# Five small edits to the attention stage: the last head pair multiplies unrounded probabilities by unrounded V in one 32-bit product per step

## The chip, the cores and the metric

The kernel runs on one core of a Trainium2 chip. The metric is the device time of one execution in microseconds (us). TensorE is called PE here, its weight loads PEld, VectorE DVE, ScalarE ACT, GpSimd POOL; SP is the engine whose queue issues most DMAs. Each engine works through its own list of instructions in order and waits on semaphores for the others.

## The reference

Three stages follow each other. The first is attention over 2 x 8 heads with 1152 keys of 64 values; pairs of neighbouring queries are averaged, so that each head has 576 queries. Then come two feed-forward layers over 1152 tokens.

```python
q_pool = q.reshape(B, H, S // 2, 2, D).mean(axis=3)
scores = scale * np.matmul(q_pool, k.transpose(0, 1, 3, 2))
attn = np.exp(scores - np.max(scores, axis=-1, keepdims=True))
attn = attn / (np.sum(attn, axis=-1, keepdims=True) + 1e-09)
x = np.matmul(attn, v)                       # then tokens x 512
h = x @ w_in                                 # layer 1, 512 -> 2048
g = (a0 + a1*h + a2*h**2 + a3*h**3) / (1 + |b0|*|h| + |b1|*h**2 + 1e-6)
x = g @ w_out                                # back to 512
h = x @ w_in2
out = softplus(h) @ w_out2                   # layer 2
```

The layers' weights come as 64-bit floats and are turned into 32-bit ones on the chip.

## The kernel before

**Rounded products.** Nearly every product runs in the rounded 32-bit format fp32r (`F32R`). To keep the accuracy, an operand is split into a rounded part and the rounded rest, as `ph` and `pl` for the probabilities `p`, and three products are added: high by high, high by low, low by high.

**Attention in pairs.** Two heads make a pair; there are 8 pairs, numbered 0 to 7, and 36 steps per pair (`ST`). A step takes 128 keys and 288 queries: `s_step` forms the scores with two products (L446, L447) and ACT takes the exponential into `p` (L450). Every two steps `s_split` casts `p` into `ph` on ACT (L457) and subtracts into `pl`, on POOL for pairs 0 to 6 and on DVE for pair 7 (L122, the line of the helper `sub`). `pv` then adds three products per step into `pv` (L469 to L471). Nine steps make a group; `xev_a` divides its result (L479 to L485: two ACT and three DVE instructions) and `xev_b` splits it into `xh` (ACT, L492) and `xl` (POOL) for layer 1.

**The maximum of the next pair.** While pair j-1 takes its steps, `p1_fill` forms the scores of pair j a first time, only for their maxima: 9 tiles of 128 queries by 3 parts of 384 keys (units `u`, 27 in all), each two products (L396), and `p1_max` reduces each on DVE (L401). Tile 4 holds the last 64 queries of one head and the first 64 of the other and takes four products. `shift_a`, `shift_t`, `shift_m` turn the maxima into ten rows of `ql` (DVE, PE L418 into `ts`, DVE L425 and L432). The PSUM buffer of `ts` is one of three that the scores `s` also use, so a later `s_step` waits until DVE has read `ts`.

**Weights.** 64 tiles of weights, 512 KB each, are loaded by SP into two buffers `wraw`, and are converted: ACT (L176), three DVE instructions (L182, L185, L188; the middle one is left out at first), then an ACT cast (L198) and a DVE subtraction (L122) into `w`. Three of them come in the middle pairs, 14 from pair 6 on, among the steps; the rest during the layers. Layer 1 begins behind pair 7: `up` forms `h` in one of two PSUM buffers (L609, 24 products for two blocks), ACT applies three functions (L625 to L627), and DVE frees the buffer with L632 to L634.

**Order.** `at(t, fn, pr)` collects the work with a due step and a priority; the sorted list is traced, and the scheduler orders each engine's list from that.

Of the kernel before, what the change touches and what calls it, by code (L numbers as in the profile page):

```python
# [7 lines left out]
F32 = mybir.dt.float32  # L8
F32R = mybir.dt.float32r
# [8 lines left out]
T = dict(  # L18
    warm=24,
    wu=1,  # L20
    ft=2,
    lv=0,
    pv=15,
    pvd=8,
    pe=8,
    ped=3,
# [8 lines left out]
    q0=27,  # L35
# [51 lines left out]
def attn_moe_kernel(tc, q, k, v, w1_in, w1_out, moe_a, moe_b, w2_in, w2_out, out):  # L87
# [210 lines left out]
    def load_v(j):  # L298
# [5 lines left out]
        )  # L304
        st["vr", j] = vr

    def prep_v(j, x):
        v2, vr = V2[j % 2][:, x], st["vr", j][:, x]
        nc.scalar.copy(out=v2[:, :, 0:64], in_=vr)
        sub(nc.gpsimd if T["vl"] > x else nc.vector, v2[:, :, 128:192], vr, v2[:, :, 0:64])  # L310
# [60 lines left out]
            nc.sync.dma_start(out=QL[j % 2][x][64:74].bitcast(F32).rearrange("p (a b) -> p a b", b=128),  # L371
                              in_=zero[64:74].bitcast(F32).unsqueeze(1).to_broadcast([10, 5, 128]))

    def p1_fill(j, u):
        t, e = divmod(u, 3)
        i = j % 2
        if u == 0:
            st["nm", j] = late.tile([128, 9, 3], F32, tag="nm", name="nm", bufs=2)
        if j == 0 and u % 2:
            o = pps.tile([128, 512], F32, tag="s", name="p1")[:, 0:384]  # L380
        else:
            o = pp1.tile([128, 512], F32, tag="p1", name="p1")[:, 0:384]
# [12 lines left out]
        for a, (l, r) in enumerate(mm):
            m = nc.tensor.matmul(out=o, lhsT=l, rhs=r, start=(a == 0), stop=(a == len(mm) - 1))  # L396
        st["last", "pe"] = m.ins

    def p1_max(j, u):
        t, e = divmod(u, 3)  # L400
        nc.vector.tensor_reduce(out=st["nm", j][:, t, e:e + 1], in_=st.pop(("p1", j, u)), axis=AX.X,  # L401
                                op=ALU.max, negate=True)
# [36 lines left out]
    def s_step(j, s):  # L439
        g, c = divmod(s, C)  # L440
        x, half = divmod(g, 2)
        i = j % 2
        cs = qcols(x, half)
        ks = slice(c * 128, (c + 1) * 128)
        t = pps.tile([128, 512], F32, tag="s", name="s")[:, 0:HALF]
        nc.tensor.matmul(out=t, lhsT=KS[i][x][:, ks], rhs=QQ[i][x][:, cs], start=True, stop=False)  # L446
        nc.tensor.matmul(out=t, lhsT=KH[x][:, ks], rhs=QL[i][x][:, cs], start=False, stop=True)  # L447
        if s % 2 == 0:
            st["p"] = late.tile([128, 2, HALF], F32, tag="p", name="p", bufs=4)
        st["last", "exp"] = nc.scalar.activation(out=st["p"][:, s % 2], in_=t, func=AF.Exp).ins  # L450

    def s_split(j, s):
        p = st["pg", j, s]
        ph = late.tile([128, 2, HALF], F32R, tag="ph", name="ph", bufs=5)
        pl = late.tile([128, 2, HALF], F32R, tag="pl", name="pl", bufs=5)
        n = s // 2 + j * ST // 2
        nc.scalar.copy(out=ph, in_=p)  # L457
        sub(nc.vector if j == NP - 1 else nc.gpsimd, pl, p, ph)
        for e in range(2):
            st["ph", j, s - 1 + e] = (ph[:, e], pl[:, e])  # L460

    def pv(j, s):
        g, c = divmod(s, C)
        if c == 0:
            st["pv", j, g] = ppv.tile([128, 512], F32, tag="wm", name="pv")[:, 0:HALF]
        ph, pl = st.pop(("ph", j, s))
        v2 = V2[j % 2][:, g // 2]
        h, l = v2[:, c, 0:128], v2[:, c, 128:192]
        nc.tensor.matmul(out=st["pv", j, g], lhsT=h, rhs=ph, start=(c == 0), stop=False)  # L469
        nc.tensor.matmul(out=st["pv", j, g][0:64], lhsT=l, rhs=ph, start=False, stop=False)  # L470
        nc.tensor.matmul(out=st["pv", j, g], lhsT=h, rhs=pl, start=False, stop=(c == C - 1))  # L471
# [16 lines left out]
    def xev_b(j, g):  # L488
        c0 = (j // NPB) * SQ + (g % 2) * HALF
        o = (slice(None), j % NPB, slice(c0, c0 + HALF))  # L490
        xs = st.pop(("xs", g % 2))
        nc.scalar.copy(out=xh[o], in_=xs)  # L492
        sub(nc.gpsimd if T["xl"] else nc.vector, xl[o], xs, xh[o])

    def s_group(j, s):
# [4 lines left out]
    for j in range(NP):  # L500
        b0, b1, b2 = ST * j, ST * (j - 1), ST * (j - 2)
        A = lambda t, fn, *a, pr=0: at(t, lambda: fn(*a), pr)
        A(b1 + T["lv"], load_v, j)
        for x in range(2):
            if j == 0:
                A(b1 + T["v0"] + T["pvd"] * x, lambda x=x: behind(lambda: prep_v(0, x), "act", "dve"), pr=7)
            else:
                if j == 1 and T["vb"]:
                    A(b1 + T["pv"] + T["pvd"] * x, lambda x=x: behind(lambda: prep_v(1, x), "act", "dves"), pr=7)
                else:  # L510
                    A(b1 + (T["pv"] + T["pvd"] * x if j < NP - 1 else T["pe"] + T["ped"] * x), prep_v, j, x, pr=7)
        if j == 0:
            A(b2 + 0, first_load)
            A(b2 + 1, warm, T["warm"])
            for f, g in FIRST:
                A(b2 + 2, f, 0, g)
                A(b1 + T["ft"], lambda f=f, g=g: behind(lambda: f(1, g), "act", "dve"))
            A(b1 + T["ft"] + 1, lambda: behind(constants, "dve"))
            A(b1 + T["ft"] + 1, lambda: behind(moe_consts, "act", "dve"))
        else:  # L520
            o = b2 + (T["k1"] if j == 1 else 0)
            A(b2 + 0, load_kq, j)
            A(o + T["pq"], prep_q, j)
            for g in range(3):
                A(o + T["tk"] + T["tkd"] * g, tr_k, j, g, pr=1)
                if j == 1 and T["tb"] > 2 - g:
                    A(o + T["tk"] + T["tkd"] * g + T["tke"],
                      lambda g=g: behind(lambda: tr_k_ev(1, g), "act", "dves"), pr=2)
                else:
                    A(o + T["tk"] + T["tkd"] * g + T["tke"], tr_k_ev, j, g, pr=2)  # L530
            for g in range(2):
                A(o + T["tq"] + T["tqd"] * g, tr_q, j, g, pr=1)
                A(o + T["tq"] + T["tqd"] * g + T["tqe"], tr_q_ev, j, g, pr=2)
            A(o + T["ks0"], dma_ks, j, 0)
            A(o + T["q0"], dma_q, j, 0)
            A(o + T["ks1"], dma_ks, j, 1)
            A(o + T["q1"], dma_q, j, 1)
        A(b0 + T["kh0"], dma_kh, j, 0)
# [10 lines left out]
            A(t0 + T["p1m"], p1_max, j, u, pr=T["prm"])  # L549
        for x in range(2):  # L550
            t0 = b1 + T["s0"] if x == 0 else b1 + T["s1"]
            A(t0, shift_a, j, x)
            A(t0 + T[f"st{x}"], shift_t, j, x, pr=1)
            A(t0 + T[f"st{x}"] + T["sm"], shift_m, j, x, pr=2)
        for s in range(ST):
            A(b0 + s, s_step, j, s, pr=0)
            if s % 2 == 1:
                A(b0 + s, s_group, j, s, pr=1)
                A(b0 + s + T["sg"], s_split, j, s, pr=T["prs"])
            g, c = divmod(s, C)  # L560
            A(b0 + C * g + T["po"] + c * T["ps"] // 9, pv, j, s, pr=T["prp"])
        for g in range(4):
            A(b0 + C * g + T["xa"], xev_a, j, g, pr=T["pra"])
            if g >= 2:
                A(b0 + C * g + T["xb"], xev_b, j, g, pr=3)

    def pre(i, t0, lead, d, pool):
        at(t0, lambda: behind(lambda: w_load(i), "sp"))
# [17 lines left out]
    tc0 = ST * (NP - 2) + T["wc"]  # L586
    at(tc0, close_early)
    at(ST * (NP - 1) + T["ce"], close_even)
    for i in range(NRA + NRB):
        pre(NE + i, tc0 + 1 + T["wg"] * i, 4, 1, (lambda: st["wra"]) if i < NRA else (lambda: st["wrb"]))  # L590

    ph_ = pa_ = ap = wl_ = pt_ = pt2 = None
# [146 lines left out]

    if True:  # L740
        make_identity(nc, ident)
        nc.vector.memset(zero, 0.0)
        for i in range(2):
            nc.gpsimd.memset(V2[i][:, :, :, 64:128].bitcast(F32), -1.0)
# [17 lines left out]
        wl_ = sb(name="wlast", bufs=NW - NP1 - NE - NRA - NRB)  # L762
        pt_ = sb(name="part", bufs=1)

        freed = [wl_] * (NW - NP1 - NE - NRA - NRB)
        n0 = NE + NRA + NRB
        cnt = {"load": n0, "abs": n0, "conv": n0, "split": n0}

        def w_step():
# [150 lines left out]
```

## Time and profile before

| what | us |
|---|---|
| median of 3 runs (748.14 to 791.52) | 749.07 |
| the profiled execution | 748.41 |
| its span, first to last instruction | 746.6 |
| PE busy in the span | 725.7 (97%) |
| DVE, ACT, POOL busy | 551.6, 502.0, 227.2 |
| scores of pairs 6 and 7 begin | 256.68, 293.09 |
| last product of pair 7 begins | 333.74 |

A busy PE is not a PE at its peak, since matmuls overlap: what one costs is read from start to start in a row without waits. The share of the whole span is an average; pairs 0 to 6, pair 7, and the layers have different limits.

### The profile page before, as it was taken

Reading aid. Unit: us, or ns where it says so; the run is one execution under the profiler, and the core shown is the slowest. Engines: PE = TensorE matmul, PEld = TensorE weight load, DVE = VectorE, ACT = ScalarE, POOL = GpSimd, SP = SyncE. Lnnn points to the kernel's source line nnn. Section 1 sums busy time; section 2 is a strip of 40 time slices with the busy share of each in tenths; the row PEclk is TensorE's granted clock in tenths of the full one; section 3 lists DMA queues with packets and bytes.
Section 4 is the critical chain, followed back from the end, with each engine's and each line's share of the span. In section 5 each row is a group of like instructions: output and inputs, shape, how many; then the busy total and the mean of one; then the engine's idle time right before and its main releaser. Section 6 shows DMA issues by size and latency. Waiting matters only on the chain.

```text
span 746.6 us, 11768 instructions
## 1 busy us (share of the span) xinstructions
PE 725.7 (97%) x4273; PEld 683.5 (92%) x4273; DVE 551.6 (74%) x956; ACT 502.0 (67%) x967; POOL 227.2 (30%) x189
## 2 busy tenths in 40 slices
PE   8999999999999998887999999999999999999998
PEld 5699999999999998777999999999899998989896
DVE  5877777777777679998989999999987575611122
ACT  3278888888888889996767777787564454422221
POOL 5278787878787776000000000000000000000000
PEclk9999999999999999998999999999999999999999
DMA  4866373737353434432111221211124333101011
GB/s 131 207 151 151 96 183 87 179 87 182 87 120 96 92 101 125 141 113 84 57 58 57 67 75 56 86 58 56 38 80 137 110 117 107 63 1 43 0 43 43
DMA packets 60475, 70.33 MB, mean 94 GB/s; under 512 B 20008, under 2 KB 48512, under 8 KB 60416
## 3 DMA queue, kind: packets, MB, share of 16 engines
q1 hardware_dynamic: 59232, 68.58, 34.0%
q10 hardware_dynamic: 1184, 0.98, 0.4%
q8 instruction: 34, 0.56, 0.3%
q14 instruction: 25, 0.20, 0.1%
HBM read 47.71 MB, written 2.36 MB: 67 GB/s over the span
## 4 chain that ended last, share of the span: by engine, by line
PE 86%; DVE 7%; ACT 5%; issue 1%; POOL 0%; DVEq 0%; ACTq 0%
PE acc L712 13%; PE h L690 13%; PE p L396 11%; PE acc L658 11%; PE h L609 11%; PE s L446 5%; PE s L447 5%; PE pv L471 4%; PE pv L469 4%; PE pv L470 4%; ACT p L450 1%; ACT ph L457 1%; PE wm L264 1%; PE tk L327 1%; DVE w L122 1%
## 5 line engine op out<-in xcount | busy, mean ns | idle before, releaser
L122 POOL TENSOR_TENSOR pl<-p,ph 128x576 fp32r<-128x576 f32 x126 | 181.5, 1453 | 54.8 <-ACT ph L457 35.4
L401 DVE TENSOR_REDUCE nm<-p 128x1 f32<-128x384 f32 x216 | 117.0, 552 | 44.4 <-PE p L396 42.9
L450 ACT ACTIVATE p<-s 128x288 f32<-128x288 f32 x288 | 114.7, 407 | 29.2 <-PE s L447 27.6
L122 DVE TENSOR_TENSOR gl<-p,gh 128x384 fp32r<-128x384 f32 (+1 forms) x72 | 49.6, 689 | 93.3 <-ACT gh L699 92.3
L609 PE MATMUL h<-xh,w 128*128 128x384 f32 x384 | 100.8, 341 | 4.2 <-DVE p L633 4.2
L457 ACT CAST ph<-p 128x576 fp32r<-128x576 f32 x144 | 96.7, 671 | 2.4
L690 PE MATMUL h<-xh,w 128*128 128x384 f32 x384 | 97.8, 336 | 0.0
L698 ACT ACTIVATE p<-h 128x384 f32<-128x384 f32 x48 | 23.6, 492 | 109.5 <-PE h L690 109.4
L658 PE MATMUL acc<-gh,w 128*128 128x384 f32 x384 | 93.0, 337 | 1.0 <-ACT gh L619 1.0
L712 PE MATMUL acc<-w,gh 128*128 128x512 f32 x288 | 90.0, 394 | 0.0
L471 PE MATMUL pv<-pl,v 128*128 128x288 f32 x288 | 87.1, 303 | 1.7 <-DVE pl L122 1.3
L469 PE MATMUL pv<-ph,v 128*128 128x288 f32 x288 | 87.1, 303 | 1.2 <-ACT ph L457 1.0
L470 PE MATMUL pv<-ph,v 128*64 128x288 f32 x288 | 85.8, 298 | 0.0
L609 PEld LDWEIGHTS h<-xh,w 128*128 128x128 f32 x384 | 71.1, 192 | 4.5 <-issue 4.5
L690 PEld LDWEIGHTS h<-xh,w 128*128 128x128 f32 x384 | 70.2, 188 | 3.9
L658 PEld LDWEIGHTS acc<-gh,w 128*128 128x128 f32 x384 | 68.7, 188 | 2.1 <-ACT gh L619 2.0
L609 PE MATMUL h<-xl,w 128*128 128x384 f32 x192 | 65.3, 340 | 0.0
L690 PE MATMUL h<-xl,w 128*128 128x384 f32 x192 | 64.6, 337 | 0.0
L712 PEld LDWEIGHTS acc<-w,gh 128*128 128x128 f32 x288 | 53.5, 188 | 9.0
L658 PE MATMUL acc<-gl,w 128*128 128x384 f32 x192 | 59.7, 338 | 0.3 <-DVE gl L122 0.3
L471 PEld LDWEIGHTS pv<-pl,v 128*128 128x128 f32 x288 | 55.0, 191 | 5.0 <-DVE pl L122 3.9
L469 PEld LDWEIGHTS pv<-ph,v 128*128 128x128 f32 x288 | 55.6, 193 | 2.6 <-ACT ph L457 2.4
(152 smaller groups left out, 1620.6 us busy)
## 6 DMA issues: line engine op xcount, KB each, us to landing
wraw<-in_moe_w_in_dram SPq DMA_DIRECT2D x32, 512.0 KB
wraw<-in_moe_w_out_dram SPq DMA_DIRECT2D x32, 512.0 KB
vr<-in_v_dram SPq DMA_DIRECT2D x8, 576.0 KB
kr<-in_k_dram SPq DMA_DIRECT2D x15, 288.0 KB
qr<-in_q_dram SPq DMA_DIRECT2D x15, 256.0 KB
out_dram<-m SPq DMA_DIRECT2D x15, 128.0 KB
kha<-ks0a SPq DMA_DIRECT2D x4, 288.0 KB
khb<-ks0b SPq DMA_DIRECT2D x4, 288.0 KB
```

Of the source, the lines that this page charges most:

```text
L122: return eng.tensor_tensor(out=o, in0=a, in1=b, op=ALU.subtract)
L396: m = nc.tensor.matmul(out=o, lhsT=l, rhs=r, start=(a == 0), stop=(a == len(mm) - 1))
L401: nc.vector.tensor_reduce(out=st["nm", j][:, t, e:e + 1], in_=st.pop(("p1", j, u)), axis=AX.X, op=ALU.max, negate=True)
L450: st["last", "exp"] = nc.scalar.activation(out=st["p"][:, s % 2], in_=t, func=AF.Exp).ins
L457: nc.scalar.copy(out=ph, in_=p)
L469: nc.tensor.matmul(out=st["pv", j, g], lhsT=h, rhs=ph, start=(c == 0), stop=False)
L470: nc.tensor.matmul(out=st["pv", j, g][0:64], lhsT=l, rhs=ph, start=False, stop=False)
L471: nc.tensor.matmul(out=st["pv", j, g], lhsT=h, rhs=pl, start=False, stop=(c == C - 1))
L609: nc.tensor.matmul(out=h, lhsT=w[:, wi, wd], rhs=x[:, d, xcols(c)], start=(n == 0), stop=(n == 3 * ND - 1))
L658: nc.tensor.matmul(out=st["acc", c, d], lhsT=w[:, wi, wd], rhs=g, start=(first and n == 0), stop=(last and n == 2))
L690: nc.tensor.matmul(out=h, lhsT=w[:, wi, d * 128:(d + 1) * 128], rhs=x[:, d, xcols(c)], start=(n == 0), stop=(n == len(mm) - 1))
L712: nc.tensor.matmul(out=st["acc", c, t], lhsT=g[:, t * 128:(t + 1) * 128], rhs=w[:, wi], start=(first and n == 0), stop=(last and n == 2))
```

## The change

1. In pair 7 `s_step` writes the exponential into buffers with the tag `ph`, and `s_split` does nothing more. `pv` issues one product per step with both operands in plain 32-bit (`F32`), V from the new tiles `vf`. `load_vf` fills five of these straight from memory (V in columns 0 to 63, -1 in 64 to 127) in buffers of `p` and `pl`, which pair 7 has no other use for; the load and the split of V into `V2` fall away for pair 7.
2. Tile 4 of `p1_fill` takes three products for pairs 1 to 7, with the two heads' queries on the diagonal of the tiles `QD`, which four DMAs per pair fill (`dma_qd`); and tile 4 comes first (`unit`).
3. The three `shift` steps of pair 7 are traced in a high priority.
4. In pair 7 `pv`, `xev_a` and `xev_b` are due earlier, and the cast into `xh` is on POOL.
5. 13 weights in place of 14 are converted ahead of layer 1's start; the buffer of the 14th is the first to be used there.

```diff
+    QD = [late.tile([128, 128], F32R, name=f"qd{x}") for x in "hl"]
...
+    def load_vf(i):
+        b, h = (NP - 1) // NPB, 2 * ((NP - 1) % NPB)
+        if i < 4:
+            t = late.tile([128, 2, HALF], F32, tag="p", name="p", bufs=4)
+        else:
+            t = late.tile([128, 2, HALF], F32, tag="pl", name="pl", bufs=5)
+        t = t.rearrange("p a b -> p (a b)")[:, 0:512].rearrange("p (c e) -> p c e", c=4)
+        nc.gpsimd.memset(t[:, :, 64:128], -1.0)
...
+                nc.sync.dma_start(
+                    out=t[:, a - n0:z - n0, 0:64],
+                    in_=v[b, h + x].rearrange("(p c) d -> p c d", p=128)[:, a - x * C:z - x * C],
+                )
+        st["vf", i] = t
...
+    def dma_qd(j):
+        for d, n in zip(QD, ("qhi", "qlo")):
+            fcopy(d[0:64, 0:64], st[n, j][0:64, 512:576])
+            fcopy(d[64:128, 64:128], st[n, j][64:128, 0:64])
+
+    def unit(j, u):
+        return u if j == 0 else u + 12 if u < 3 else u - 3 if u < 15 else u
...
+        if j and t == 4:
+            mm = [(QD[0], st["khi", j][:, ks]), (QD[0], st["klo", j][:, ks]), (QD[1], st["khi", j][:, ks])]
+            srcs = []
...
         if s % 2 == 0:
-            st["p"] = late.tile([128, 2, HALF], F32, tag="p", name="p", bufs=4)
+            if j == NP - 1:
+                st["p"] = late.tile([128, 2, HALF], F32, tag="ph", name="ph", bufs=5)
+            else:
+                st["p"] = late.tile([128, 2, HALF], F32, tag="p", name="p", bufs=4)
...
     def s_split(j, s):
         p = st["pg", j, s]
+        if j == NP - 1:
+            for e in range(2):
+                st["ph", j, s - 1 + e] = (p[:, e], None)
+            return
...
-        sub(nc.vector if j == NP - 1 else nc.gpsimd, pl, p, ph)
+        sub(nc.gpsimd, pl, p, ph)
...
+        if j == NP - 1:
+            n = (g // 2) * C + c
+            nc.tensor.matmul(out=st["pv", j, g], lhsT=st["vf", n // 4][:, n % 4], rhs=ph, start=(c == 0), stop=(c == C - 1))
+            return
         nc.tensor.matmul(out=st["pv", j, g], lhsT=h, rhs=ph, start=(c == 0), stop=False)
...
-        nc.scalar.copy(out=xh[o], in_=xs)
+        if j == NP - 1:
+            nc.gpsimd.tensor_copy(out=xh[o], in_=xs)
+        else:
+            nc.scalar.copy(out=xh[o], in_=xs)
...
+            f = high if j == NP - 1 else lambda fn, *a: fn(*a)
+            A(t0, f, shift_a, j, x)
+            A(t0 + T[f"st{x}"], f, shift_t, j, x, pr=1)
+            A(t0 + T[f"st{x}"] + T["sm"], f, shift_m, j, x, pr=2)
...
-    for i in range(NRA + NRB):
+    for i in range(NRA + NRB - 1):
```

Line numbers of the changed kernel differ: its score products are L482 and L483, its product for pair 7 L514, ACT's first function of layer 1 L682, the DVE rows that write `ql` L461 and L468, `p1_max` L437, and the weights' cast and first ACT function L202 and L180.

**PE in the middle of pair 7's second head.** Before:

```order
L446 MATMUL s<-qq1b,ks1b 128x288
L447 MATMUL s<-ql1b,khb 128x288
L471 MATMUL pv<-pl,v_110 128x288
L469 MATMUL pv<-ph,v_110 128x288
L470 MATMUL pv<-ph,v_110 64x288
L471 MATMUL pv<-pl,v_110 128x288
L446 MATMUL s<-qq1b,ks1b 128x288
L447 MATMUL s<-ql1b,khb 128x288
```

Now:

```order
L483 MATMUL s<-ql1b,khb 128x288
L514 MATMUL pv<-ph,p 128x288
L482 MATMUL s<-qq1b,ks1b 128x288
L483 MATMUL s<-ql1b,khb 128x288
L514 MATMUL pv<-ph,p 128x288
L482 MATMUL s<-qq1b,ks1b 128x288
```

A step was two score products and three products with V, in a changing order; it is now two and one, strictly in turn, and the product with V (here `p` is the `vf` tile) trails the scores by four steps.

**DVE where the shift of pair 7's first head is written.** Before:

```order
L401 TENSOR_REDUCE nm<-p_4359 128x1
L188 SCALAR_TENSOR_TENSOR pk<-wraw,pk 128x512
L122 TENSOR_TENSOR w<-pk,w 128x512
L401 TENSOR_REDUCE nm<-p_4387 128x1
L425 TENSOR_TENSOR ql1a<-ts,mask 10x512
L432 TENSOR_SCALAR ql1a<-ts,mask 10x64
```

Now:

```order
L437 TENSOR_REDUCE nm<-p_4364 128x1
L192 SCALAR_TENSOR_TENSOR pk<-wraw,pk 128x512
L126 TENSOR_TENSOR w<-pk,w 128x512
L461 TENSOR_TENSOR ql1a<-ts,mask 10x512
L468 TENSOR_SCALAR ql1a<-ts,mask 10x64
L437 TENSOR_REDUCE nm<-p_4392 128x1
```

One reduction moved from ahead of the two shift instructions to behind them; the two weight instructions still stand ahead.

**ACT between the end of pair 7 and layer 1.** Before:

```order
L492 CAST xh<-xs_4699 128x288
L479 ACTIVATE xr<-pv,eps 64x288
L480 ACTIVATE xr<-xr 64x288
L198 CAST w<-pk 128x512
L492 CAST xh<-xs_4817 128x288
L176 ACTIVATE pk<-wraw 128x512
L625 ACTIVATE p<-h,a_sb 128x768
```

Now:

```order
L526 ACTIVATE xr<-pv,eps 64x288
L527 ACTIVATE xr<-xr 64x288
L202 CAST w<-pk 128x512
L180 ACTIVATE pk<-wraw 128x512 x2
L682 ACTIVATE p<-h,a_sb 128x768
```

The two casts into `xh` left ACT's list, and with them the wait of the second one for DVE's `xs` ahead of layer 1's first function.

## Rows read from the trace of the kernel before

**Rows 1.** Windows: from:to, length, busy us (x instructions) per engine, clock, DMA share, GB/s.

```profile
80.00:100.00 20.00, 20.00 (x142) 19.62 (x141) 15.63 (x33) 17.28 (x41) 15.95 (x14) 1.00 0.55 134
293.09:333.87 40.78, 36.47 (x209) 30.83 (x208) 38.03 (x69) 39.04 (x89) 5.34 (x4) 0.92 0.43 137
311.15:329.20 18.05, 15.84 (x94) 12.50 (x93) 16.96 (x31) 17.88 (x42) 0.00 (x0) 1.00 0.42 137
341.00:345.14 4.14, 0.00 (x0) 0.00 (x0) 2.92 (x4) 4.14 (x6) 0.00 (x0) 0.84 0.49 151
345.14:350.70 5.56, 5.53 (x17) 5.56 (x18) 5.56 (x7) 4.65 (x8) 0.00 (x0) 0.51 0.00 0
360.00:380.00 20.00, 20.00 (x117) 20.00 (x116) 17.78 (x23) 14.87 (x21) 0.00 (x0) 1.00 0.16 54
```

**Rows 2.** Timeline of PE in pair 1: start us, us, engine, line, operation.

```profile
83.53 0.29 PE L469 MATMUL pv<-ph,v 128*128 128x288 f32 x1
...
84.19 0.34 PE L396 MATMUL p<-ks0a,qq0a 128*128 128x384 f32 x1
...
84.89 0.30 PE L469 MATMUL pv<-ph,v 128*128 128x288 f32 x1
...
85.56 0.49 PE L327 MATMUL tk<-ident,kr 128*128 128x128 f32 x3
85.80 0.42 PE L396 MATMUL p<-ks0a,qq0a 128*128 128x384 f32 x1
```

**Rows 3.** Timeline at the shift of pair 7; brackets: idle before, and its releaser.

```profile
288.06 1.92 DVE L122 TENSOR_TENSOR w<-pk,w 128x512 fp32r<-128x512 f32 x1
...
289.90 0.54 DVE L401 TENSOR_REDUCE nm<-p 128x1 f32<-128x384 f32 x1
...
290.46 0.68 DVE L425 TENSOR_TENSOR ql1a<-ts,mask 10x512 fp32r<-10x512 f32 x1
...
291.48 0.37 PE L446 MATMUL s<-qq0b,ks0b 128*128 128x288 f32 x1 [1.87 <-DVE ql1a L432]
```

**Rows 4.** Timeline of ACT in pair 7.

```profile
314.12 0.67 ACT L457 CAST ph<-p 128x576 fp32r<-128x576 f32 x1
...
314.69 0.42 ACT L450 ACTIVATE p<-s 128x288 f32<-128x288 f32 x1
...
314.99 0.68 ACT L176 ACTIVATE pk<-wraw 128x512 f32<-128x512 f32 x1
...
315.56 0.41 ACT L450 ACTIVATE p<-s 128x288 f32<-128x288 f32 x1
...
316.41 0.64 ACT L198 CAST w<-pk 128x512 fp32r<-128x512 f32 x1
...
316.94 0.73 ACT L450 ACTIVATE p<-s 128x288 f32<-128x288 f32 x2
```

**Rows 5.** Groups by line and form: count, busy us, mean ns, idle before.

```profile
L469 PEld LDWEIGHTS pv<-ph,v 128*128 128x128 f32 x288 | 55.6, 193 | 2.6 <-ACT ph L457 2.4
...
L479 ACT ACTIVATE xr<-pv,eps 64x288 f32<-64x288 f32 x32 | 16.0, 499 | 4.5 <-PE pv L471 4.0
```

**Rows 6.** Timeline from pair 7 into layer 1.

```profile
330.66 0.33 PE L609 MATMUL h<-xh,w 128*128 128x384 f32 x1
...
332.91 0.51 PE L609 MATMUL h<-xh,w 128*128 128x384 f32 x2
...
333.74 0.29 PE L471 MATMUL pv<-pl,v 128*128 128x288 f32 x1
...
338.63 0.43 ACT L492 CAST xh<-xs 128x288 fp32r<-128x288 f32 x1 [2.88 <-DVE xs L485]
...
339.70 1.00 ACT L625 ACTIVATE p<-h,a_sb 128x768 f32<-128x768 f32 x1
...
342.22 0.96 DVE L632 TENSOR_TENSOR p<-h,p 128x768 f32<-128x768 f32 x1 [1.25 <-ACT s L627]
...
345.17 0.98 PE L609 MATMUL h<-xh,w 128*128 128x384 f32 x2 [4.20 <-DVE p L633]
```

More of the change, by code (lines that the diff above doesn't have):

```diff
@@ L116, in behind, with high @@
             fn()
+    def high(fn, *a):
+        with tc.high_priority():
+            fn(*a)
     def sb(**kw):
@@ L305, in load_v @@
         st["vr", j] = vr
+    def load_vf(i):
[6 more added lines that the diff above has]
+        nc.gpsimd.memset(t[:, :, 64:128], -1.0)
+        n0, n1 = 4 * i, min(4 * i + 4, 2 * C)
+        for x in range(2):
+            a, z = max(n0, x * C), min(n1, x * C + C)
+            if a < z:
+                nc.sync.dma_start(
[3 more added lines that the diff above has]
+        st["vf", i] = t
     def prep_v(j, x):
@@ L372, in dma_q, with p1_fill @@
                               in_=zero[64:74].bitcast(F32).unsqueeze(1).to_broadcast([10, 5, 128]))
-    def p1_fill(j, u):
+    def dma_qd(j):
[4 more added lines that the diff above has]
+        return u if j == 0 else u + 12 if u < 3 else u - 3 if u < 15 else u
+    def p1_fill(j, n):
+        u = unit(j, n)
         t, e = divmod(u, 3)
         i = j % 2
-        if u == 0:
+        if n == 0:
             st["nm", j] = late.tile([128, 9, 3], F32, tag="nm", name="nm", bufs=2)
@@ L397, in p1_fill, with p1_max @@
         st["last", "pe"] = m.ins
-    def p1_max(j, u):
+    def p1_max(j, n):
+        u = unit(j, n)
         t, e = divmod(u, 3)
@@ L502, in attn_moe_kernel @@
         A = lambda t, fn, *a, pr=0: at(t, lambda: fn(*a), pr)
-        A(b1 + T["lv"], load_v, j)
+        if j < NP - 1:
+            A(b1 + T["lv"], load_v, j)
+        else:
+            for i in range(5):
+                A(b0 - 1 + 2 * i, load_vf, i, pr=9)
         for x in range(2):
@@ L510, in attn_moe_kernel @@
                 else:
-                    A(b1 + (T["pv"] + T["pvd"] * x if j < NP - 1 else T["pe"] + T["ped"] * x), prep_v, j, x, pr=7)
+                    if j < NP - 1:
+                        A(b1 + T["pv"] + T["pvd"] * x, prep_v, j, x, pr=7)
         if j == 0:
@@ L535, in attn_moe_kernel @@
             A(o + T["q0"], dma_q, j, 0)
+            A(o + T["q0"], dma_qd, j)
             A(o + T["ks1"], dma_ks, j, 1)
@@ L551, in attn_moe_kernel @@
             t0 = b1 + T["s0"] if x == 0 else b1 + T["s1"]
-            A(t0, shift_a, j, x)
-            A(t0 + T[f"st{x}"], shift_t, j, x, pr=1)
-            A(t0 + T[f"st{x}"] + T["sm"], shift_m, j, x, pr=2)
+            f = high if j == NP - 1 else lambda fn, *a: fn(*a)
+            A(t0, f, shift_a, j, x)
+            A(t0 + T[f"st{x}"], f, shift_t, j, x, pr=1)
+            A(t0 + T[f"st{x}"] + T["sm"], f, shift_m, j, x, pr=2)
         for s in range(ST):
@@ L560, in attn_moe_kernel @@
             g, c = divmod(s, C)
-            A(b0 + C * g + T["po"] + c * T["ps"] // 9, pv, j, s, pr=T["prp"])
+            A(b0 + C * g + (T["po"] if j < NP - 1 else 4) + c * T["ps"] // 9, pv, j, s, pr=T["prp"])
         for g in range(4):
-            A(b0 + C * g + T["xa"], xev_a, j, g, pr=T["pra"])
+            A(b0 + C * g + (T["xa"] if j < NP - 1 else 13), xev_a, j, g, pr=T["pra"])
             if g >= 2:
-                A(b0 + C * g + T["xb"], xev_b, j, g, pr=3)
+                A(b0 + C * g + (T["xb"] if j < NP - 1 else 16), xev_b, j, g, pr=3)
     def pre(i, t0, lead, d, pool):
@@ L741, in attn_moe_kernel @@
         make_identity(nc, ident)
+        for d in QD:
+            nc.gpsimd.memset(d.bitcast(F32), 0.0)
         nc.vector.memset(zero, 0.0)
@@ L763, in attn_moe_kernel @@
         pt_ = sb(name="part", bufs=1)
-        freed = [wl_] * (NW - NP1 - NE - NRA - NRB)
-        n0 = NE + NRA + NRB
+        freed = [st["wrb"]] + [wl_] * (NW - NP1 - NE - NRA - NRB)
+        n0 = NE + NRA + NRB - 1
         cnt = {"load": n0, "abs": n0, "conv": n0, "split": n0}
```

## The prediction

> **What bounds the kernel now.** I read the page's slices first (PE 9 nearly everywhere, with a hole around 340 us), then windows by stage, then the timeline where the edits lie. In pairs 0 to 6 PE has no free time: 20.00 of 20.00 us, with DVE, ACT and POOL at 78 to 86% [rows 1]. There a matmul less is time less, and work taken from another engine is worth nothing. In pair 7 it is otherwise: no maxima of a next pair are formed, weights are converted in among the steps, and ACT is busy 17.88 of 18.05 us while PE has holes (15.84) [rows 1]. Its two heads take equally long, 18.05 us for 18 steps. Behind it lies the hole: PE does nothing from 341.00 to 345.14 and then runs at a granted clock of 0.51, the 1.2 GHz level, until 350.70 [rows 1]. The reader is to see there that PE waits for DVE L633, DVE's first instruction waited for ACT L627, and ACT began layer 1 only at 339.70, since in its list the cast into `xh` stood ahead and waited 2.88 us for DVE's `xs` [rows 6]. From 345.14 on DVE has no gap either (5.56 of 5.56) [rows 1].
>
> **Prices.** From start to start in a row without waits: a product of 288 columns 0.132 us (five from 83.53 to 84.19), one of 384 columns 0.175 (the four of a tile-4 unit, 84.19 to 84.89) [rows 2], in layer 1 0.171 (117 in 20.00) [rows 1]. On ACT: the cast into `ph` 0.57 (314.12 to 314.69), an exponential 0.30, the first function of a weight 0.57, its cast 0.53 [rows 4].
>
> **1. Tile 4.** 3 units in each of 7 pairs lose one product: 21 x 0.175 = 3.7 us, all of it on PE's full list. The 28 small DMAs that replace it go through SP's queue ahead of loads that are due later, with the DMA engines at 0.55 [rows 1]; I cost them at nothing. If that cover is gone, a pair's first tile waits. **-3.7.**
>
> **2. The shift of pair 7.** PE stood 1.87 us for `ql1a`. One reduction of 0.56 (289.90 to 290.46) leaves its way; the weight subtraction of 1.92 us still stands ahead [rows 3]. Bounds 0 and 1.87. **-0.55.**
>
> **3. Pair 7.** From its first score (293.09) to the end of its last product (333.87) it takes 40.8 us [rows 1]; in it lie 8 products of layer 1 (from 330.66 to the two of 332.91 [rows 6]), 1.4 us, which leaves 39.4. Now, on PE: 18 products left over from pair 6 (2.4), 72 score products (9.5), and 36 products in plain 32-bit. No row shows one. The nearest below are the plain 32-bit transposes: three in 0.24 us (85.56 to 85.80), 0.08 for 128 columns, so 0.18 for 288 [rows 2]. The nearest above is four products that nothing overlaps, each as dear as the one behind a wait, 0.37 [rows 3]: 1.48. I take 0.53, four times 0.132: this kernel needs three rounded products to come near one exact one, the fourth, low by low, left out, and a unit that multiplies what these rows show would have to do all four. A transpose moves values and need not multiply them, so I trust it less. 36 x 0.53 = 19.1, with the rest 31.0 us.
> The Trainium skill ("FP8 and Floating Point Precision", TensorE Precision Notes) says that true FP32 takes four passes through the array, high and low parts against each other. By that rule the sum stays at mine; by the row of the transposes it would be the first rival's. No row here can settle it.
> ACT would need less: 36 exponentials (10.8), ten weights at 1.10 (11.0), five divisions at two times 0.50 [rows 5] (5.0), a last cast of pair 6 and two into `xh` (1.5): 28.3. Before, 18 casts of 0.57 stood on top, 10.3 us, and made ACT the bound. DVE loses its 18 subtractions as well. The first V tiles wait for two memsets on POOL, among pair 6's last subtractions, and for SP, but the product that needs them trails the scores by four steps. For such starts, for waits between PE and ACT and for a stretch at the lower clock (the window's mean is 0.92 [rows 1]) I add 2.5 us: an estimate, bounds 0 and 5. 39.4 - 31.0 - 2.5: **-5.9.**
>
> **4. The start of layer 1.** Without its 8 early products pair 7's end would be 332.5; DVE's first instruction followed at 342.22, 9.7 us later. Now it is 24 products of `up` (4.1) and ACT's three functions, 339.70 to 342.22 (2.5) [rows 6]: 6.6. The casts into `xh` on POOL delay only tokens that come blocks later, and POOL is idle. **-3.1.** PE then has most of its hole and of the low clock back, but I count nothing for it: DVE was full from 345.14 on and its work for layer 1 is the same, so what PE gains ahead of DVE it waits for again; at most the 2.2 us that DVE is free from 360 to 380 [rows 1].
>
> **5. At nothing:** the dropped split of V (POOL, ACT and DVE in pair 6, where PE is the bound) and the 14th weight, which moves into layer 1 and is covered by that same slack of DVE; if not, about its 1.1 us on ACT again on DVE.
>
> **Sum:** 748.41 - 3.7 - 0.55 - 5.9 - 3.1 = 735.2, against the profiled execution, which is 0.66 below the median of the three runs.
>
> **Rivals.**
> *One pass.* The plain 32-bit product costs 0.18, as the transposes. Then PE needs 18.4 us in pair 7, ACT's 28.3 and the 2.5 are the bound, 30.8: 2.7 less than mine, 732.5.
> *Weights pace pair 7.* ACT's list is in order; if a weight's 512 KB, two buffers and its DVE steps cannot come faster than now, exponentials wait behind L176's successor and pair 7 keeps its 39.4. Against it: DMA share 0.42, DVE loses work [rows 1]. 748.4 - 7.35 = 741.1.
> *Loads in the open.* Each of four parts needs weights of its own, and a load takes 0.193 [rows 5], today under the product before. Four in a row: 0.77, pair 7 takes 11.9 + 27.7 + 2.5 = 42.1, 743.8.
> *Slower.* Nothing overlaps in the new product: 1.48 each, pair 7 takes 11.9 + 53.3 + 2.5 = 67.7, 28.3 more than now; with the 7.35 of the other edits 769.4. It eats the gain from 0.90 us per product on, and is over 2% slower from 1.33 on. For it: each product alternates with two of another format. Against: nothing in these rows costs more than 0.37.
>
> **Numbers.** 2%, about what a measurement of this kernel can tell from no change, is 15 us: faster means below 734.1, slower above 764.1, by the median 749.07. My case, 731 to 739 with the bounds of its terms, gets 0.56, and four tenths of it lie below 734.1; one pass 0.14 (faster), weights 0.13 and loads 0.11 (no change by that measure), slower 0.06. Faster 0.22 + 0.14 = 0.36, same 0.34 + 0.24 = 0.58, slower 0.06. The time is my case's, 735.2. The range leaves out the slow rival and the tails: 727 is one pass without the 2.5 and with DVE's 2.2, rounded; 748 the open loads with the margin doubled and one more wait.
>
> **What would show it.** Units of tile 4 with three products and pairs 0 to 6 each some 0.5 us shorter; PE's wait for `ql1a` about 1.3 us; a new product every 0.79 us in pair 7, 0.53 behind its start to the next score, with PE, not ACT, at 90% or more; ACT L682 about 4 us behind pair 7's last product, with no wait for `xs` ahead of it; and the first window of 20 us in layer 1 with DVE full. I am wrong if the new product's spacing is far from 0.53, or if ACT waits for weights in pair 7.

## The result: 0.9% faster, less than half of what was forecast

| | us |
|---|---|
| before, median of 4 runs | 749.02 |
| changed, median of 4 runs (742.11 to 743.03) | 742.47 |
| ratio, 95% interval | 0.9914 [0.9899, 0.993] |
| profiled execution of the changed kernel, its span | 742.58, 740.7 |
| forecast (range 727 to 748) | 735.2 |

One of the four runs before (791.52 us) and one of the four of e2 below (754.12) were slow, and the ratios are of the other runs alone.

The sign and the range held, the size didn't: 5.8 us between the two profiled executions where 13.2 were forecast. Cut at the same places as the prediction's sum, the two traces give:

| stretch | before | changed | measured | forecast |
|---|---|---|---|---|
| start to the first score of pair 0 | 33.51 | 33.71 | +0.2 | 0 |
| pairs 0 to 6, to the first score of pair 7 (terms 1 and 2) | 259.58 | 256.35 | -3.2 | -4.25 |
| pair 7 without products of layer 1 (term 3) | 39.4 | 35.2 | -4.2 | -5.9 |
| from there to DVE's first instruction of layer 1 (term 4) | 9.7 | 10.1 | +0.4 | -3.1 |
| from there to the end of the span | 404.4 | 405.3 | +0.9 | 0 |

### The profile page after: what moved, and what is told of

The parts are those of the page before. It is cut to its first block, busy times and chain, and to the rows that moved or that the text cites. A ratio compares the mean times of both kernels' runs of the same rounds, so it can differ in the third digit from the quotient of the medians.

```text
span 740.7 us, 11685 instructions
## 1 busy us (share of the span) xinstructions
PE 719.3 (97%) x4216; PEld 677.0 (91%) x4216; DVE 543.4 (73%) x938; ACT 491.0 (66%) x945; POOL 228.9 (31%) x197
## 4 chain that ended last, share of the span: by engine, by line
PE 81%; DVE 10%; ACT 4%; issue 3%; DMA 1%; POOL 0%; DVEq 0%; ACTq 0%; SPq 0%
PE acc L769 14%; PE h L747 13%; PE p L431 10%; PE h L666 9%; PE acc L715 9%; PE s L482 5%; PE s L483 5%; PE pv L518 4%; PE pv L516 4%; PE pv L517 4%; PE pv L514 3%; PE wm L269 1%; DMA wraw<-in_moe_w_in_dram 1%; DVE p L689 1%; DVE m L691 1%
## 5 line engine op out<-in xcount | busy, mean ns | idle before, releaser
L437 DVE TENSOR_REDUCE nm<-p 128x1 f32<-128x384 f32 x216 | 116.2, 553 | 47.8 <-PE p L431 45.6
L489 ACT ACTIVATE p<-s 128x288 f32<-128x288 f32 x252 | 100.8, 407 | 28.2 <-PE s L483 26.7
L500 ACT CAST ph<-p 128x576 fp32r<-128x576 f32 x126 | 84.6, 671 | 2.3
L518 PE MATMUL pv<-pl,v 128*128 128x288 f32 x252 | 74.8, 297 | 1.1 <-POOL pl L126 1.1
L516 PE MATMUL pv<-ph,v 128*128 128x288 f32 x252 | 75.2, 299 | 0.0
L517 PE MATMUL pv<-ph,v 128*64 128x288 f32 x252 | 74.3, 295 | 0.0
L769 PE MATMUL acc<-w,gl 128*128 128x512 f32 x144 | 56.9, 395 | 0.0
L518 PEld LDWEIGHTS pv<-pl,v 128*128 128x128 f32 x252 | 47.5, 188 | 1.9 <-POOL pl L126 1.6
```

The lines of the kernel that those rows point to most:

```text
L769: nc.tensor.matmul(out=st["acc", c, t], lhsT=g[:, t * 128:(t + 1) * 128], rhs=w[:, wi], start=(first and n == 0), stop=(last and n == 2))
```

## The profile after

Windows of the changed kernel, columns as in [rows 1]: pair 7, the stretch behind a wait in it, a stretch of its steady part, PE's work of layer 1 ahead of its hole, the hole, and what follows.

```profile
290.06:325.20 35.14, 31.54 (x164) 26.49 (x163) 27.87 (x51) 28.82 (x70) 6.13 (x8) 0.95 0.53 156
...
296.76:300.00 3.24, 3.24 (x10) 2.74 (x11) 2.20 (x3) 2.34 (x6) 0.83 (x1) 0.54 0.63 152
302.00:310.00 8.00, 8.00 (x44) 6.64 (x43) 6.63 (x14) 7.61 (x19) 0.95 (x1) 1.00 0.40 138
...
325.28:334.01 8.73, 8.72 (x50) 8.35 (x48) 6.79 (x12) 4.13 (x8) 3.35 (x4) 1.00 0.56 159
334.01:338.37 4.36, 0.00 (x0) 0.03 (x1) 3.00 (x5) 4.36 (x7) 0.00 (x0) 0.88 0.56 166
338.37:345.00 6.63, 6.63 (x23) 6.63 (x24) 6.63 (x9) 4.76 (x7) 0.00 (x0) 0.57 0.00 0
```

Where pair 7 runs undisturbed, PE is full (8.00 of 8.00 us) and ACT nearly (7.61): PE is the bound there, as the second head before was not [rows 1]. But two stretches spoil it. Over all of pair 7 PE misses 3.6 us, and behind that gap it runs at the 1.2 GHz level. And the hole ahead of layer 1, 4.14 us before, is still there with 4.36.

The timeline of PE in the steady part (start, us, engine, line, operation):

```profile
302.05 0.65 PE L514 MATMUL pv<-ph,p 128*128 128x288 f32 x2
302.32 0.51 PE L482 MATMUL s<-qq1a,ks1a 128*128 128x288 f32 x1
302.67 0.30 PE L483 MATMUL s<-ql1a,kha 74*128 74x288 f32 x1
302.81 0.65 PE L514 MATMUL pv<-ph,p 128*128 128x288 f32 x2
...
305.08 0.65 PE L514 MATMUL pv<-ph,p 128*128 128x288 f32 x2
```

Four steps take 3.03 us, 0.757 each. Without the two score products (2 x 0.132, their price elsewhere) the 32-bit product costs **0.49 us**. The trace shows each as two records: 72 records in pair 7 for 36 products.

The wait ahead of the first of these products (brackets: idle before, and its releaser):

```profile
290.77 1.68 POOL L126 TENSOR_TENSOR pl<-p,ph 128x576 fp32r<-128x576 f32 x1 [1.41 <-ACT ph L500]
...
291.17 1.83 DVE L192 SCALAR_TENSOR_TENSOR pk<-wraw,pk 128x512 int32<-128x512 int32 x1
...
292.79 1.49 POOL L126 TENSOR_TENSOR pl<-p,ph 128x576 fp32r<-128x576 f32 x1
292.93 1.87 DVE L446 CAST s<-m 128x5 fp32r<-128x5 f32 x1
...
294.47 0.31 POOL L319 MEMSET p<- 128x256 f32 x1
294.83 0.46 DVE L528 SCALAR_TENSOR_TENSOR xm<-pv,xr 64x288 f32<-64x288 f32 x1
...
296.21 0.45 DVE L532 SCALAR_TENSOR_TENSOR xs<-xm,pv 64x288 f32<-64x288 f32 x1
...
296.76 1.30 PE L514 MATMUL pv<-ph,p 128*128 128x288 f32 x2 [3.19 <-issue]
```

PE stands 3.19 us with no releaser named ("issue"), but it starts as DVE's L532 ends (296.66). That is the last instruction of the division of pair 6's third group, which frees one of the two PSUM buffers for the sums. The division comes late since DVE spends 3.6 us on L192 and L446, a weight step and a cast of five columns. Both lie beside a subtraction of POOL, and L446 ends with POOL's last memset for a V tile (294.78); with nothing of POOL beside them L192 takes 0.69 and L446 0.16 to 0.17. The rival reading is the load of the first V tile.

The way into layer 1, for comparison with [rows 6]:

```profile
325.28 0.72 PE L666 MATMUL h<-xh,w 128*128 128x384 f32 x2
...
328.03 0.37 SPq L166 DMA_DIRECT2D wraw<-in_moe_w_in_dram  x1
...
332.21 0.67 ACT L180 ACTIVATE pk<-wraw 128x512 f32<-128x512 f32 x1 [3.02 <-DMA wraw<-in_moe_w_in_dram]
...
332.90 0.99 ACT L682 ACTIVATE p<-h,a_sb 128x768 f32<-128x768 f32 x1
...
335.42 0.96 DVE L689 TENSOR_TENSOR p<-h,p 128x768 f32<-128x768 f32 x1 [1.36 <-ACT s L684]
...
338.37 0.98 PE L666 MATMUL h<-xh,w 128*128 128x384 f32 x2 [4.37 <-DVE p L690]
```

No wait for `xs` stands ahead of ACT's first function any more, as forecast. In its place ACT waits 3.02 us for a weight's load, issued at 328.03, whose conversion its list puts ahead of L682; the 24 products that it needs had begun at 325.28 and the last of them at 329.5. L682 starts 7.6 us behind pair 7, not 4.

## Experiments

In all of them the kernel before ran on the same chip; its median was 748.6 to 748.8.

**e1: ACT's first block of layer 1 ahead of the weights.**

```diff
-        nc.scalar.activation(out=s, in_=h, func=AF.Square)
+        e = nc.scalar.activation(out=s, in_=h, func=AF.Square)
+        st.setdefault(("last", "a1"), e.ins)
...
-                w_step()
+                behind(w_step, "a1")
```

> The changed kernel with ACT's first block of layer 1 (L682 to L684) put ahead of the two weight conversions that stood in front of it in ACT's list; nothing is left out. Theory A (the weight's load, 3.02 us of wait in ACT's list, took the place of the wait for xs): L682 begins at about 329.7 in place of 332.90, DVE's first instruction of layer 1 at 332.2 in place of 335.42, PE's hole shrinks from 4.37 us to about 1.2, and the kernel takes 739.5 +- 0.5. Theory B (DVE is the bound from there on and its work is the same, so that the place of ACT's functions is worth little): the hole shrinks, but PE waits for DVE later, and the kernel takes 741.5 to 742.5.

739.4 us, ratio 0.9879 [0.9863, 0.9895]. ACT, DVE and PE in its timeline:

```profile
330.40 0.99 ACT L682 ACTIVATE p<-h,a_sb 128x768 f32<-128x768 f32 x1 [3.21 <-PE h L666]
...
332.92 0.96 DVE L690 TENSOR_TENSOR p<-h,p 128x768 f32<-128x768 f32 x1 [3.09 <-ACT s L684]
...
335.87 0.59 PE L666 MATMUL h<-xh,w 128*128 128x384 f32 x2 [1.35 <-DVE p L691]
```

The hole is 1.35 us, PE keeps 2.4 GHz behind it, and the whole 3.1 us show in the time. Theory A: the weight's load stood in the place of the wait removed. The start of layer 1 is now 7.1 us (325.8 to 332.92) against the 6.6 forecast.

**e2: the shift of pair 7's second head in ordinary order.**

```diff
-            f = high if j == NP - 1 else lambda fn, *a: fn(*a)
+            f = high if j == NP - 1 and x == 0 else lambda fn, *a: fn(*a)
```

> The changed kernel with the shift of pair 7's second head back in ordinary order (the first head's stays in high priority): on DVE the division of pair 6's third group then stands ahead of the shift's two small instructions, of which the cast took 1.87 us. Theory A (PE's 3.19 us without work ahead of pair 7's first product with V is a wait for the sum's buffer, which DVE frees late): the wait shrinks to about 1.3 us, the stretch at 1.2 GHz behind it gets shorter, and the kernel takes 739.5 to 741. Theory B (the wait is for the first V tile's load or memset): the wait stays at 3.2 and the kernel at 742.5.

739.33 us, ratio 0.9879 [0.9861, 0.9896]. The division on DVE and PE behind it:

```profile
292.97 0.46 DVE L528 SCALAR_TENSOR_TENSOR xm<-pv,xr 64x288 f32<-64x288 f32 x1
...
293.91 0.82 DVE L446 CAST s<-m 128x5 fp32r<-128x5 f32 x1
...
294.77 0.45 DVE L532 SCALAR_TENSOR_TENSOR xs<-xm,pv 64x288 f32<-64x288 f32 x1
...
295.32 0.72 PE L514 MATMUL pv<-ph,p 128*128 128x288 f32 x2 [1.81 <-issue]
```

L532 ends 1.4 us earlier and PE's wait is 1.4 us shorter; the first V tile's load is issued when it was (287.0 us, 287.1 in the changed kernel). So PE waits for the sum's buffer, and the high priority of the second head's shift, which put its cast ahead of the division, made that late: this half of edit 3 costs the changed kernel 3.1 us. Only part of them comes from PE's wait: pair 7 gets 0.6 us shorter, since PE now waits for ACT at its end; the hole of layer 1 falls from 4.37 to 2.67.

**e5: both repairs** (the two diffs together).

> The changed kernel with both repairs: ACT's first block of layer 1 ahead of the two weight conversions, and the shift of pair 7's second head in ordinary order. Alone each took 3.1 us off. Theory A (two separate waits): both gains stand, 742.5 - 6.2, about 736.3. Theory B (the gain of the shift came for 1.7 us through the hole at layer 1, 4.37 to 2.67, which the other repair closes as well): PE waits 1.8 us ahead of pair 7's first product, the hole is 1.2 to 1.4, and the kernel takes 738 +- 0.5.

738.04 us, ratio 0.9856 [0.9836, 0.9875]: theory B to the tenth, the two gains share the hole.

**e6: a rounded product in its place, on e1's kernel.**

```diff
...
-            n = (g // 2) * C + c
-            nc.tensor.matmul(out=st["pv", j, g], lhsT=st["vf", n // 4][:, n % 4], rhs=ph, start=(c == 0), stop=(c == C - 1))
+            nc.tensor.matmul(out=st["pv", j, g], lhsT=h, rhs=ph, start=(c == 0), stop=(c == C - 1))
...
```

> The kernel of e1 with the one product per step of pair 7 in the rounded format: probabilities and V are rounded, and the rest of neither is multiplied, which leaves out a part of the accuracy; V comes through the split of pairs 0 to 6 again, without the V tiles. The product then costs 0.13 us in place of 0.49. Theory A (PE bounds pair 7, its product for 36 x 0.36 = 13 us more than ACT's need of 28.3): pair 7 falls from 34.8 us to some 30, PE waits for ACT, and the kernel takes 735 to 736. Theory B (the weights' loads and conversions pace pair 7 and the start of layer 1): pair 7 gets shorter, what it gains goes into waits for weights, and the kernel takes 738.5 to 739.5. It also tells the wait ahead of pair 7's first product apart once more: without V tiles it stays near 3 us if it is for DVE's division.

737.88 us, ratio 0.9854 [0.9835, 0.9874], 1.5 below e1, between the two theories. Two of PE's waits in pair 7:

```profile
296.32 0.37 PE L513 MATMUL pv<-ph,v 128*128 128x288 f32 x1 [2.74 <-DVE xs L531]
...
302.89 0.40 PE L482 MATMUL s<-qq1a,ks1a 128*128 128x288 f32 x1 [0.64 <-ACT ph L489]
```

Pair 7 falls to 32.0 us (290.28 to 322.28), 3.6 less than in e1 and far less than the 13 us that PE saves, since ACT takes over as the bound (busy 9.67 of 10.00 us from 300 to 310). By the traces 2.8 are given back behind DVE's first instruction of layer 1 (404.2 us to the end in e1, 406.9 here), where PE has a second hole of 1.33 us; the rest of it was not found. Without any V tile the first product still waits 2.74 us, now with DVE's division as the named releaser. The 0.45 us that it waits less than in e1 are those of DVE's cast, which in e6 ends with POOL's subtraction, since no memset follows:

```profile
292.78 1.51 POOL L126 TENSOR_TENSOR pl<-p,ph 128x576 fp32r<-128x576 f32 x1 [0.31 <-POOL pl L126]
292.94 1.38 DVE L446 CAST s<-m 128x5 fp32r<-128x5 f32 x1
```

**e8: the last two subtractions of pair 6 on DVE.**

```diff
-        sub(nc.gpsimd, pl, p, ph)
+        sub(nc.vector if j == NP - 2 and s >= 33 else nc.gpsimd, pl, p, ph)
```

> The changed kernel with the last two subtractions of pair 6 on DVE in place of POOL. Theory A (DVE's weight step of 1.83 us and its cast of 5 columns of 1.87 us, ahead of the division, are slow because POOL subtracts at the same time): they take 0.7 and 0.2 to 0.3 us, and the last fp32r subtractions of DVE itself 0.7 to 0.8. Theory B (they are slow by themselves or by a DMA): they still take over 1.5 us each. DVE has 1.5 us more to do there, and the last products of pair 6 wait for it: for the time of the kernel 741 to 744 by either theory.

739.66 us, ratio 0.9877 [0.9855, 0.99]. The same two DVE instructions, and the product:

```profile
291.02 0.68 DVE L192 SCALAR_TENSOR_TENSOR pk<-wraw,pk 128x512 int32<-128x512 int32 x1
...
291.62 0.16 DVE L446 CAST s<-m 128x5 fp32r<-128x5 f32 x1
...
294.56 0.72 PE L514 MATMUL pv<-ph,p 128*128 128x288 f32 x2 [0.16 <-issue]
```

Theory A: 1.83 becomes 0.68, 1.87 becomes 0.16, and DVE does two more subtractions (0.75 each) and is still earlier. The wait falls from 3.19 to 0.16 us (with 0.7 more just ahead of it for `pl`), the clock stays at 1.00 to 300 us, and pair 7 takes 32.6 us (289.92 to 322.53). By theory the kernel's time was to be 741 to 744: the gain was underestimated.

**e3: the tile-4 edit alone, on the kernel before.**

```diff
...
+        if j and t == 4:
+            mm = [(QD[0], st["khi", j][:, ks]), (QD[0], st["klo", j][:, ks]), (QD[1], st["khi", j][:, ks])]
+            srcs = []
...
```

> The kernel before with edit 2 alone (tile 4 with three products, first in order, with its four small loads per pair). Theory A (in pairs 0 to 6 a product less is time less): 21 x 0.175 = 3.7 us, 745.3. Theory B (other waits take a part of it back, as the starts of the pairs of the changed kernel suggest, which came forward by 0.3 to 0.5 us each): 2.4 us or less, 746.5 to 748.

745.57 us, ratio 0.9964 [0.9949, 0.9978], 3.0 us, between the two theories. Pairs 1 to 5 are shorter by 0.47, 0.58, 0.57, 0.59 and 0.48, mean 0.54 against 0.525 forecast. Pair 0 is only 0.07 shorter and pair 6 is 0.07 longer, so that pairs 0 to 6 gain 2.7. In each of these two a wait appears that the kernel before did not have:

```profile
37.72 0.40 PE L485 MATMUL pv<-pl,v 128*128 128x288 f32 x1 [0.65 <-POOL pl L122]
```

```profile
278.17 0.44 PE L409 MATMUL p<-ks1b,qq1b 128*128 128x384 f32 x1 [1.10 <-DVE nm L415]
```

**e4 and e12: three rounded products again, then the cast into `xh` back on ACT.** e4 undoes edit 1 and the earlier due steps of edit 4; e12 changes one more line, so that pair 7 takes the branch of the other pairs:

```diff
-        if j == NP - 1:
+        if j == NP:
             nc.gpsimd.tensor_copy(out=xh[o], in_=xs)
         else:
```

> The changed kernel with edit 1 undone and, with it, the earlier due steps of edit 4: three rounded products per step in pair 7, with the split of V and the casts and subtractions of the probabilities. Theory A (the 32-bit product saves what pair 7 got shorter by, 39.4 to 35.2 us): pair 7 back at about 39.5 us, the kernel at 746 to 747. Theory B (the waits that came with it ate the gain, and the rest comes from the other edits): 742 to 743.

> The kernel of e4 (three rounded products in pair 7) with the cast into xh back on ACT. Theory A (with a long pair 7 the cast on POOL takes the wait for xs out of ACT's list, and that is worth the 3 us forecast for the start of layer 1): from the end of pair 7 to DVE's first instruction of layer 1 6.5 us becomes some 9.5, and the kernel takes 747 to 747.5. Theory B (the cast's engine is worth nothing, the order of the weights makes e4's start short): 744.5.

e4 744.45 us, ratio 0.9949 [0.9935, 0.9962], between the two theories; e12 749.88, ratio 1.0018 [1.0009, 1.0026], 2.4 above theory A. Both traces at the start of layer 1, e4 first:

```profile
335.57 0.99 ACT L667 ACTIVATE p<-h,a_sb 128x768 f32<-128x768 f32 x1
...
338.09 0.96 DVE L674 TENSOR_TENSOR p<-h,p 128x768 f32<-128x768 f32 x1 [0.62 <-ACT s L669]
...
338.89 0.68 ACT L180 ACTIVATE pk<-wraw 128x512 f32<-128x512 f32 x1 [0.83 <-DMA wraw<-in_moe_w_in_dram]
```

```profile
338.25 0.43 ACT L532 CAST xh<-xs 128x288 fp32r<-128x288 f32 x1 [2.04 <-DVE xs L522]
...
339.69 0.66 ACT L180 ACTIVATE pk<-wraw 128x512 f32<-128x512 f32 x1 [1.00 <-DMA wraw<-in_moe_w_in_dram]
340.38 0.99 ACT L667 ACTIVATE p<-h,a_sb 128x768 f32<-128x768 f32 x1
...
342.89 0.96 DVE L674 TENSOR_TENSOR p<-h,p 128x768 f32<-128x768 f32 x1 [1.36 <-ACT s L669]
...
345.85 0.98 PE L651 MATMUL h<-xh,w 128*128 128x384 f32 x2 [5.18 <-DVE p L675]
```

From pair 7's last product (332.64 in e4, 333.61 in e12) to DVE's first instruction of layer 1 it takes 5.5 and 9.3 us. The 3.8 between them are not the price of the cast alone: with its engine the order of ACT's list changed too, and the weight's conversion (L180) that stands ahead of L667 in e12 stands behind it in e4 (338.89). In e12 the cast ends at 338.68 and the weight's load holds ACT until 339.69. So e4 shows the start of layer 1 with neither in the way, and that is term 4 as it was meant: counted as before, without its nine early products of layer 1 (1.5 us), e4 has 6.8 where 6.6 were forecast. e12 loses more, 5.4 in all: 0.9 lies ahead of pair 0, where nothing differs, and behind its hole of 5.18 us PE runs at a granted clock of 0.50 to 352 us, where e4, with a hole of 1.35, keeps 1.00.

e4 is also the price of edit 1 in the changed kernel. Pair 7 is 41.2 us there (290.01 to 332.77, less the early products) against 35.2, 6.0 saved; but from e4 to the changed kernel only 2.0 us remain, since the start of layer 1 goes from 6.8 back to 10.1. The 41.2 are 1.8 more than in the kernel before: here too the division of pair 6's third group ends late, ACT waits for it, and PE for ACT:

```profile
295.95 0.43 ACT L532 CAST xh<-xs 128x288 fp32r<-128x288 f32 x1 [2.23 <-DVE xs L522]
...
296.74 0.40 PE L482 MATMUL s<-qq1a,ks1a 128*128 128x288 f32 x1 [1.60 <-ACT p L487]
```

**e7: 14 weights ahead of layer 1 again.**

```diff
-    for i in range(NRA + NRB - 1):
+    for i in range(NRA + NRB):
...
```

> The changed kernel with edit 5 undone: 14 weights ahead of layer 1. Theory A (the weights come at the pace of their loads either way, and ACT has the same two conversions ahead of its first function): 742.5 +- 0.5. Theory B (a weight less ahead of layer 1 takes its 1.1 us off ACT there): 743.5.

741.96 us, ratio 0.9907 [0.9882, 0.9932]: no difference that can be told. The hole is 4.60.

**e9, e10, e11: e1's order with two, four and ten subtractions of pair 6 on DVE** (`s >= 33`, `29`, `17` in e8's line).

> The changed kernel with the last two subtractions of pair 6 on DVE and ACT's first block of layer 1 ahead of the two weight conversions. Theory A (the wait ahead of pair 7's first product, 3.19 us, and the weight load's wait at layer 1 are separate, and each repair gains its own): 739.7 - 3.1 = 736.6, with a hole of 1.35 us. Theory B (DVE or the weights bound what follows): 738 or more, as e5.

> As e9, with the last four subtractions of pair 6 on DVE. Theory A (the shift of pair 7 comes late because its weight subtraction, 1.92 us, runs beside POOL's): that subtraction takes 0.7, PE's wait of 1.2 us for ql1a goes, and the kernel takes 735.5. Theory B (DVE has 0.75 us more for each, and is at 11.84 of 12.00 us there): the shift comes no earlier, other products of pair 6 wait for DVE, and the kernel takes 737 or more.

> As e9, with the last ten subtractions of pair 6 on DVE. Theory A (PE's wait of 1.1 us for a maximum at 277 us, which gave back pair 6's share of the tile-4 gain, comes from DVE's steps of 1.4 to 1.9 us beside POOL): it goes as well, 734.5. Theory B (DVE becomes the bound of pair 6's second half): 738 or more, with PE waiting for DVE's maxima or for pl.

| | us | ratio, 95% interval |
|---|---|---|
| e9 | 736.15 | 0.9835 [0.9822, 0.9849] |
| e10 | 735.31 | 0.9824 [0.981, 0.9837] |
| e11 | 735.17 | 0.9822 [0.9808, 0.9835] |

e9 is theory A: two separate waits, each with its own gain. In e10 the wait for `ql1a` is gone as well, by this row on DVE, which read 1.92 us in the changed kernel:

```profile
285.69 0.68 DVE L126 TENSOR_TENSOR w<-pk,w 128x512 fp32r<-128x512 f32 x1
```

In e11 the wait of 1.10 us in pair 6 goes too, and pair 6 takes 33.24 us (36.01 in the changed kernel). But pair 7 is 0.7 us longer than in e10, with waits of 0.8 and 1.0 us for DVE and ACT, and the last 1.0 us that is left at the start of layer 1 is given back before the end of the span (733.4 against 733.5): theory A for the wait, not for the time. e10 and e11 beat both kernels by more than their intervals.

## Why the prediction was wrong, point by point

**Term 1 (-3.7; measured 3.0 alone, 2.7 of it in pairs 0 to 6).** The price of a product was right in five pairs of seven (0.54 against 0.525). "In pairs 0 to 6 PE has no free time" was read from one window of 20 us in pair 1; in pair 0 POOL and in pair 6 DVE stand next, and PE waited for them as soon as it had less to do. e11 shows the latter: with POOL's subtractions off DVE's way the wait goes.

**Term 2 (-0.55; measured 0.67, from 1.87 to 1.20; e3, without edit 3, has 1.66).** Right for the shift of pair 7's first head. Edit 3 moved that of the second head too, and the term puts that at nothing: it costs 3.1 us (e2). The weight subtraction of 1.92 us that "still stands ahead" [rows 3] could have been asked why it takes three times its usual 0.68.

**Term 3 (-5.9; measured 4.2).** The product's price was right, 0.49 against 0.53, and with it PE as the bound and both far bounds, 0.18 and 1.48, wrong. The Trainium skill ("FP8 and Floating Point Precision", TensorE Precision Notes) speaks of four passes for true FP32; by that rule an estimate is 4 x 0.132 = 0.53, and the time agrees within 8%, though the trace shows two records per product and no passes. PE's need is 2.4 + 9.5 + 36 x 0.49 = 29.5 us, so pair 7 took 5.7 more than that. Too small was the margin of 2.5 "for such starts, for waits between PE and ACT and for a stretch at the lower clock": the one wait of 3.19 us and the 3.24 us at a mean clock of 0.54 behind it, worth 1.5 us, are 4.7. The place was seen, but the main resource was not named: of the memsets and loads of the V tiles that the prediction names, the loads had no part and the memsets 0.45 us (e6). A product that is due earlier also needs its sum's buffer earlier, and that hung on DVE's division of the group before, which edit 3 and POOL's subtractions made late. e2, e6 and e8 show it; with e8 pair 7 takes 32.6 us, better than the forecast 33.5.

**Term 4 (-3.1; measured +0.4). This is the step that failed most**: "Now it is 24 products of `up` (4.1) and ACT's three functions". It took the wait for `xs` out of ACT's list and did not ask what else stands there: a weight's conversion, ahead of L625 in the order before and ahead of L682 in the order now. Its load ended at about the same time as the wait that the prediction saw. In the kernel before:

```profile
335.05 6.35 SPq L162 DMA_DIRECT2D wraw<-in_moe_w_in_dram  x3
...
339.01 0.67 ACT L176 ACTIVATE pk<-wraw 128x512 f32<-128x512 f32 x1
```

By the order of the two buffers, this weight's load is the one issued at 335.05, 2.6 us behind pair 7 (332.5). In e3, e4, e12 and the changed kernel ACT starts such a conversion, behind a wait for its load, 4.0 to 4.2 us after the issue; by that, an estimate, the load landed here at about 339.0, as the cast into `xh` ended (339.06). In the changed kernel its counterpart is issued 2.75 us behind pair 7 (328.03) and ends the wait at 332.21. So two waits ended together ahead of layer 1's first function, and the term took out one. It is not the shorter pair 7 that lengthened the other: in e8, where pair 7 is 2.6 us shorter still, it is 2.92 us. The rival "weights pace pair 7" had this mechanism with 0.13, at the wrong place: the weights did not hold the exponentials, but the function behind the last of them. In e4 and e1, where no weight stands ahead of the function, the start takes 6.8 and 7.1 us: the term's sum is right, what stands in ACT's list was missed.

**Term 5 (0).** e7 agrees, as far as 0.3% can tell.

**DVE's slack.** "What PE gains ahead of DVE it waits for again" was no limit for e1, whose 3.1 us all stayed: what was moved forward there was DVE's own first instruction. Where the changed kernel loses its 0.9 us behind it was not found; the low clock is no answer, since the kernel before has a like stretch there (5.56 us at 0.51 [rows 1], here 6.63 at 0.57).

The sum had its parts nearly right for a kernel in which nothing new waits: e10, where the three waits are gone, takes 735.3, and cut as in the table above it has -4.2, -6.2 and -2.6 where -4.25, -5.9 and -3.1 were forecast. That it meets the forecast is still in part luck: its subtractions on DVE and its order of the weights are not in the change, and the sum did not price them.

## What to carry to other kernels

When a term takes a wait out of an in-order list, read the next entries of that list, and ask of each what it waits for after all the other terms have come true: here a load ended in the same moment as the wait that was taken out, and so showed no wait of its own. When work is pulled forward, list every buffer that it needs, the output's too, and who frees it. An instruction that takes three times its usual time on the critical path is worth a look at what the other engines do in the same microsecond.

## What the hardware showed unexpectedly

**DVE beside POOL.** While POOL subtracts from and to SBUF (1.4 to 1.85 us each), DVE's weight step took 1.83 us in place of 0.68, its subtraction 1.92 in place of 0.68, and a cast of five columns 1.87 in place of 0.16; reductions and the division, which read PSUM, kept their 0.55 and 0.46. Taking POOL's subtractions away (e8, e10) brings the short times back. The Trainium skill ("SBUF — State Buffer", Who interferes with whom) says that a DVE instruction with two inputs in SBUF contends with a POOL instruction that reads SBUF, that a copy or cast in a mode with two ports contends with POOL as well, and that whoever issues first holds the shared ports for its whole instruction while the other is blocked. The trace agrees: DVE's weight step ends at 293.00, 0.55 us behind POOL's first subtraction (292.45). The cast ends at 294.80, 0.52 behind the second subtraction (294.28) but 0.02 behind the last memset (294.78), and in e6, which has no memset there, 0.03 behind the subtraction. It is the plainest case: of its 16 executions in the changed kernel the seven with nothing of POOL beside them take 0.16 to 0.17 us, the nine others 0.23 to 1.87.

**The clock behind a wait.** Behind PE waits of 1.81 us (e2, e5), 2.74 (e6) and more the granted clock fell to 0.50, the 1.2 GHz level, for some microseconds (6.15 behind e12's 5.18); behind those of 1.05 to 1.35 us (e1, e4, e9, e10) it stayed at 1.00. Between these both happened: it fell 2.5 us behind e4's wait of 1.60 us and did not fall behind e3's of 1.66. In the kernel before it also fell from 306.2 to 309.7 us, with no wait over 0.53 us shortly before. So a wait that is shortened a little can gain more than its own length, but its length alone does not tell.
